# Reordering one core's instruction streams: batch 2's transposes, block 3's weight sums, and single copies and products

## The chip, the cores and the metric

One core of a Trainium2 chip runs the kernel. The metric is device time in microseconds of one execution; runs shown as times are medians. The engines are TensorE (PE, with its weight loads as PEld), VectorE (DVE), ScalarE (ACT), GpSimd (POOL) and SyncE (SP), whose queue issues most DMAs. Each engine executes its own instructions strictly in the order in which the kernel writes them, and waits on semaphores for the others.

## The reference

Eight batches of eight heads (sequence 576, head dimension 64) pass through a decayed linear attention; the result, 4608 tokens of width 512, goes through a feed-forward layer with a "snake" activation.

```python
scores = scale * np.matmul(q, k.transpose(0, 1, 3, 2))
Dmat = np.where(rel >= 0, gamma[:, None, None] ** rel[None, :, :], 0.0)
ret = scores * Dmat[None, :, :, :]
x = np.matmul(ret, v)              # to (tokens, 512)
h = x @ w_in                       # 512 -> 2048
s = np.sin(alpha * h)
g = h + s * s / (alpha + 1e-09)
out = g @ w_out                    # 2048 -> 512
```

## The kernel before

**Attention of one batch.** Queries and keys are loaded as float32 (`load`, L110, on SP's queue; the slots of the "raw" buffer are six), scaled by powers of gamma and cast to float16 (`cast`, L138, on DVE, POOL or ACT), and transposed: batches 0 and 1 on PE (`turn`, L209, then a copy out of PSUM, `take`), later batches by a DMA transpose on SP's queue (`crossed`, L201, L205). The 512 first tokens are cut into four chunks of 128. `outer` (L285, L298) makes the sum of key times value of each chunk; `evict` or `evict_bank` copies it from PSUM; `more` and `to_state` (L332 to L340, POOL) run the decayed sum over the chunks and cast the state. `scores` (L348, L358), `masked` (L366, L370, DVE), `values` (L378, L400) and `add_states` (L411, L422) give the output, which `keep` copies to `xT`. `values` is called twice for each half of the tokens (`same` false, then true), in matmuls on the two halves of the array's rows that write one bank. Between the two calls PE is drained (`change_rows`), or, with `relay`, a mark is queued on another engine that waits for the first group, and the second group waits for the mark (`told`, `order`).

**Feed-forward of one block of 512 tokens.** A unit is one of 16 slices of 128 of the 2048 hidden features. `project` (L527, L535) multiplies it on PE into a PSUM bank, `sine` (L540, ACT), `square` (L548, ACT mostly, DVE or POOL) and `product` (L557, L559, DVE) apply the activation and write `gT`; with the product the bank comes free. For blocks 0 and 1 `gemm2` (L576, L581) multiplies with `w_out` in 16 steps of four matmuls, and `finish` copies and stores. From block 2 on, class `Quarters` saves one of eight products of the second multiplication in the manner of Strassen and Winograd: weights are summed once (`weigh`, L602, POOL), and the activations of a block are summed as follows, each in two halves (0 and 1):

- `s3` (L618): a difference into the tile `d3`; read by `s2` and by multiplication 7
- `s1` (L621): in place; read by multiplication 5
- `s2` (L624) and `s4` (L630), both on POOL: in place; read by multiplications 1, 6 and 2, 3

`multiply` (L634, L652) makes one of the seven products; `add` (L665, L672, DVE) joins a product in PSUM with a stored sum and `store` writes out.

**Order.** Everything is written out by hand. Blocks 0 to 2 with the attention of batches 1 to 4 are one long list of calls (L750 to L1261). Blocks 3 to 7 come from a loop (L1276) in which the second multiplication of block n-1 (`Q`), the activation of block n (`N`), the scores and values of batch n+1 (`A`) and the casts, transposes and outer products of batch n+2 (`B2`) are laid between 16 units; the loop has conditions on `n == 3`, because block 3 follows the hand-written list. Three banks (h0, h1, h2) take turns for the units of the loop, so that unit u+3 needs the bank that the product of unit u frees. The bank "op" takes the second multiplication: multiplications 5 and 3 of one block fill it, an addition reads it, and multiplication 1 of the next block fills it anew.

Of the kernel before, what the change touches and what calls it, by code (L numbers as in the profile page):

```python
# [18 lines left out]
def kernel(  # L19
# [68 lines left out]
    V, A_, G_ = nc.vector, nc.scalar, nc.gpsimd  # L88
# [459 lines left out]
    def square(n, fc, eng):  # L548
        s_t = hps_of[n, fc][1]
        ss_t = work.tile([P, 512], F16, tag="ss", bufs=4, name="ss_t")  # L550
        if eng is nc.scalar:
            nc.scalar.activation(ss_t, s_t, mybir.ActivationFunctionType.Square)  # L552
        else:
            eng.tensor_tensor(ss_t, s_t, s_t, MULT)
        hps_of[n, fc][1] = ss_t

    def product(n, fc):  # L557
        hps, ss_t = hps_of.pop((n, fc))
        nc.vector.scalar_tensor_tensor(  # L559
            gT[n][:, :, fc, :], ss_t.rearrange("p (t n) -> p t n", t=2), inva[:, fc : fc + 1],  # L560
            hps.rearrange("p (t n) -> p t n", t=2), MULT, ADD,
        )
# [13 lines left out]
    def gemm2(n, u, tag, cols=slice(0, 512)):  # L576
        c, part = divmod(u, 4)
        if (n, c, cols.start) not in ops:
            ops[n, c, cols.start] = psum.tile([P, 512], F32, tag=tag, bufs=1, name="ops")
        for fk in range(4 * part, 4 * part + 4):  # L580
            matmul(  # L581
                ops[n, c, cols.start][:, cols], gT[n][:, c // 2, fk, c % 2 * P : c % 2 * P + P], w_out16[:, fk, cols],
                start=(fk == 0), stop=(fk == FC - 1), skip_group_check=True,
            )
# [102 lines left out]
    at = [Attention(b) for b in range(B)]  # L687
# [52 lines left out]
    with tc.manual_schedule():  # L740
# [139 lines left out]
        project(0, 11, "op")  # L880
        sine(0, 11)
        square(0, 11, V)
        product(0, 11)
        product(0, 10)
        turn(1, "k", 0, "m1")
        project(0, 12, "h2")
        sine(0, 12)
# [26 lines left out]
        at[1].scores(0, 1, "m1")  # L914
        at[1].masked(0, 0)
        at[1].masked(0, 1)
        gemm2(0, 13, "h2")
        cast(1, "v", 0, G_, (0,))
        cast(1, "v", 0, A_, (1,))
        load_w_out(2)  # L920
        load_w_out(3)
        gemm2(0, 1, "h0")
        load(2, "k", 1)
        load(2, "k", 0)
        load(2, "q", 0)
        at[1].outer((0,), "m0")
        at[1].evict((0,), A_)
        cast(1, "k", 1, G_)
        at[1].to_state(0, G_)
        at[1].values(0, False, "m1")  # L930
        at[1].values(0, True)
        turn(1, "k", 1, "h1")
        take(1, "k", 1, A_)
# [37 lines left out]
        finish(0, 1)  # L971
        cast(2, "q", 0, V)
        crossed(2, 0, "q")
        load(3, "k", 1)
        at[1].more(3)
        at[1].to_state(3, G_)
# [11 lines left out]
        sine(1, 1)  # L988
        gemm2(0, 3, "h0")
        product(1, 0)  # L990
        square(1, 1, A_)
        finish(0, 0)
        project(1, 2, "m1", 0)
        project(1, 2, "m1", 1)
        sine(1, 2)
# [1 line left out]
        square(1, 2, A_)  # L997
        project(1, 3, "h0")
        sine(1, 3)
        load(3, "q", 1)  # L1000
        load(3, "v", 0)
        crossed(2, 1, "k")
        crossed(2, 1, "q")
        load(3, "k", 0)
        load(3, "v", 1)
        load(3, "q", 0)
# [15 lines left out]
        sine(1, 6)  # L1022
        square(1, 6, A_)
        at[2].outer((0, 1), "op", "h2")
        at[2].evict_bank(0, V)
        project(1, 7, "h0", 0)
        project(1, 7, "h0", 1)
        at[2].evict_bank(1, V)
        project(1, 8, "h1", 0)
        project(1, 8, "h1", 1)  # L1030
        sine(1, 8)
# [204 lines left out]
        sine(2, 13)  # L1236
        square(2, 13, A_)
        product(2, 13)
        second[2].s3(1, V)
        sine(2, 14)  # L1240
        square(2, 14, A_)
        sine(2, 12)
        square(2, 12, V)
        product(2, 14)
        product(2, 12)
        project(2, 10, "h2", 0)
        project(2, 10, "h2", 1)
# [28 lines left out]
        for n in range(3, NBLK):  # L1276
            A = at[n + 1] if n < 7 else None
            B2 = at[n + 2] if n < 6 else None
            Q, N = second[n - 1], second[n]
            if n == 7:  # L1280
                E = (Ends(0), Ends(2))

            def scores(p):
                if A:
                    A.scores(p, 0, next(m))
                    A.scores(p, 1, next(m))
                elif n == 7 and p == 1:
                    E[0].scores(next(m))
                    E[1].scores(next(m))

            def masked(p, y):
                if A:
                    A.masked(p, y)
                elif n == 7 and p == 1:
                    E[y].masked()

            def values():
                if n == 7:
                    for e in E:
                        e.values(False, next(m))  # L1300
                    for e in E:
                        e.values(True)
                        e.add_states()
                    for e in E:
                        e.keep(0, A_)
                        e.keep(1, A_)
                if not A:
                    return
                relay = A_ if B2 else None
                A.values(0, False, next(m), relay=relay)  # L1310
                A.values(1, False, next(m), relay=relay)
                if B2:
                    B2.outer((0, 1), "op", next(h))
                A.values(0, True)
                A.add_states(0)
                A.values(1, True)
                A.add_states(1)
                if B2:
                    B2.evict_bank(0, A_)
                A.keep(0, A_)  # L1320
                if B2:
                    B2.evict_bank(1, A_)

            def begin(u):
                project(n, u, next(h))
                sine(n, u)

            def end(u):
                on_v = (12, 13) if A else ()
                square(n, u, V if u in on_v else A_)  # L1330
                product(n, u)

            def unit(u):
                begin(u)
                end(u)

            begin(0)
            if n < 6:
                for x in KEYS[3:]:
                    load(n + 2, *x)  # L1340
            if n == 6:
                last_tokens(1, "load")
                last_tokens(2, "load")
            if n == 7:
                last_tokens(3, "cast")
            if n > 3:
                Q.s1(0, V)
                Q.s1(1, V)
            end(0)
            unit(1)  # L1350
            Q.multiply(1, "X", "op")
            Q.keep("P1", "X")
            Q.s2(0, G_)
            Q.s2(1, G_)
            unit(2)
            begin(3)
            scores(0)
            end(3)
            masked(0, 0)
            masked(0, 1)  # L1360
            Q.multiply(2, "X")
            Q.keep("C11", "X")
            Q.store("C11", 0, 0)
            ahead = 3 if n == 3 else 6
            if n < 6:
                for x in KEYS[:ahead]:
                    cast(n + 2, *x, G_)
            Q.s4(0, G_)
            Q.s4(1, G_)
            if n < 6:  # L1370
                for x in KEYS[ahead:]:
                    cast(n + 2, *x, G_)
            if n == 6:
                for j in range(3):
                    last_tokens(j, "cast")
                last_tokens(3, "load")
            unit(4)
            begin(5)
            Q.multiply(6, "Y", "op")
            Q.add("U2", "P1", "Y")  # L1380
            end(5)
            if n == 3:
                Q.s1(0, V)
            unit(6)
            unit(7)
            if n == 3:
                Q.s1(1, V)
            Q.multiply(7, "Y")
            begin(8)
            scores(1)  # L1390
            Q.add("U3", "P1", "Y")
            masked(1, 0)
            end(8)
            masked(1, 1)
            if n < 5:
                for x in KEYS[:3]:
                    load(n + 3, *x)
            if n == 5:
                last_tokens(0, "load")
            unit(9)  # L1400
            begin(10)
            Q.multiply(4, "Y")
            Q.add("P1", "P1", "Y")
            Q.store("P1", 1, 0)
            end(10)
            if B2:
                crossed(n + 2, 0, "k")
                crossed(n + 2, 1, "k")
            N.s3(0, V)
            unit(11)  # L1410
            N.s3(1, V)
            begin(12)
            values()
            end(12)
            if B2:
                B2.chain((0, 1, 2, 3))
                crossed(n + 2, 0, "q")
                crossed(n + 2, 1, "q")
            begin(13)
            if A:  # L1420
                A.keep(1, A_)
            Q.multiply(5, "Z", "op")
            Q.add("U3", "U3", "Z")
            Q.store("U3", 1, 1)
            end(13)
            unit(14)
            begin(15)
            Q.multiply(3, "Z")
            Q.add("U2", "U2", "Z")
            Q.store("U2", 0, 1)  # L1430
            end(15)

        Q = second[8]
# [60 lines left out]
```

## Time and profile before

| | |
|---|---|
| median of three runs | 300.28 us (300.15 to 300.67) |
| profiled execution | 300.5 us, of which span 298.8 us |
| PE busy | 282.0 us (94% of the span) |
| DVE, ACT, POOL busy | 220.2, 210.3, 206.3 us |
| granted PE clock, mean | 0.995 |
| DMA | 49.89 MB, mean 167 GB/s |
| chain that ended last | 73% PE, 7% DVE, 6% POOL, 6% DMA |

All times of instructions are microseconds from the start of the span of the profiled execution. Busy time of PE is modelled from pipelined matmuls, so that "busy" does not mean "at its peak"; an idle gap of PE, on the other hand, is a wait. In rows of instructions a bracket gives the engine's idle time before the instruction and what ended it. Block 3 begins near 108 us and block 4 near 140 us.

### The profile page before, as it was taken

The page shows a single profiled execution, that of the slowest core. Times are in us where ns is not written, and L with a number is a line of the kernel's source. Part 1 is how long each engine was busy: PE and PEld are TensorE (multiplying, and loading weights), DVE is VectorE, ACT ScalarE, POOL GpSimd, SP SyncE. Part 2 cuts the span into 40 slices and gives each one's busy share as a digit, 9 for nine tenths or more (in the row PEclk, how much of TensorE's full clock was granted, in tenths as well). Part 3 has the DMA queues.
Part 4 walks back from the last instruction along what each step waited for, and adds up shares of the span by engine and source line. Part 5 has one row for each costly group of instructions (what it writes and reads, how often), then busy time and mean ns, then how long its engine had stood idle before and what let it go on. Part 6 is the DMA issues. An engine that isn't in the chain of part 4 may idle for free.

```text
span 298.8 us, 8739 instructions
## 1 busy us (share of the span) xinstructions
PE 282.0 (94%) x3599; PEld 183.3 (61%) x3599; DVE 220.2 (74%) x297; ACT 210.3 (70%) x338; POOL 206.3 (69%) x201
## 2 busy tenths in 40 slices
PE   7589999998899999989999999999999999999993
PEld 5454454575544576656666666766666666665782
DVE  3868957688768997998678667776778486656871
ACT  3559742795866898776878787878777878887600
POOL 4997869999799989887897799769925900370000
PEclk9999999999999999999999999999999999999998
DMA  8999999999999767988699786476648201310225
GB/s 227 291 241 216 254 217 284 255 253 159 221 273 300 90 152 174 259 191 197 143 260 185 173 203 174 88 160 145 159 91 192 55 0 41 71 37 18 61 49 120
DMA packets 119159, 49.89 MB, mean 167 GB/s; under 512 B 69824, under 2 KB 118096, under 8 KB 119120
## 3 DMA queue, kind: packets, MB, share of 16 engines
q1 hardware_dynamic: 114528, 45.04, 65.1%
q0 software_dynamic: 4224, 4.19, 8.4%
q8 instruction: 28, 0.46, 0.7%
q10 hardware_dynamic: 368, 0.11, 0.2%
q14 instruction: 11, 0.09, 0.1%
HBM read 36.74 MB, written 9.44 MB: 155 GB/s over the span
## 4 chain that ended last, share of the span: by engine, by line
PE 73%; DVE 7%; POOL 6%; DMA 6%; ACT 3%; issue 2%; SPq 1%; POOLq 0%; ACTq 0%; DVEq 0%
PE hps L535 33%; PE hps L652 27%; PE ops L581 5%; DMA q<-in_q_dram 5%; DVE ret L370 2%; DVE gT L559 2%; POOL T L602 2%; PE sc L358 2%; PE o L400 2%; PE idle L696 1%; POOL v L104 1%; ACT s_t L543 1%; PE kv L298 1%; DMA k<-in_k_dram 1%; DVE k L181 1%
## 5 line engine op out<-in xcount | busy, mean ns | idle before, releaser
L559 DVE SCALAR_TENSOR_TENSOR gT<-ss_t,inva,hps 128x512 f16<-128x512 f16 x144 | 105.3, 744 | 42.2 <-ACT ss_t L552 39.7
L543 ACT ACTIVATE s_t<-hps,alpha_t 128x512 f16<-128x512 f32 x144 | 96.7, 680 | 39.9 <-PE hps L535 39.6
L535 PE MATMUL hps<-xT,w_in 128*128 128x512 f16 (+1 forms) x592 | 121.3, 350 | 3.2 <-DVE gT L559 2.8
L535 PEld LDWEIGHTS <-w_in 128*128 128x128 f16 x656 | 62.8, 98 | 54.5 <-issue 4.3
L552 ACT ACTIVATE ss_t<-s_t 128x512 f16<-128x512 f16 x119 | 74.5, 630 | 3.3
L652 PEld LDWEIGHTS <-gT 128*128 128x128 f16 x656 | 63.9, 98 | 14.4
L624 POOL TENSOR_TENSOR gT<-gT,d 128x1024 f16<-128x1024 f16 x12 | 25.2, 2123 | 29.7 <-PE hps L652 28.6
L652 PE MATMUL hps<-T,gT 128*128 128x256 f16 x336 | 39.8, 273 | 0.0
L652 PE MATMUL hps<-w_out,gT 128*128 128x256 f16 x320 | 38.2, 273 | 0.0
L370 DVE TENSOR_TENSOR ret<-sc,mask 128x1024 f16<-128x1024 f32 (+1 forms) x32 | 34.9, 1115 | 3.0 <-PE sc L358 2.9
L672 DVE TENSOR_TENSOR osb<-osb,hps 128x512 f32<-128x512 f32 x35 | 24.0, 685 | 15.4 <-PE hps L652 14.7
L581 PE MATMUL ops<-w_out,gT 128*128 128x512 f16 x128 | 30.8, 380 | 0.0
L181 POOL TENSOR_TENSOR q<-q,cn 128x1024 f16<-128x1024 f32 (+1 forms) x16 | 25.7, 1622 | 1.5 <-DMA q<-in_q_dram 1.4
L630 POOL TENSOR_TENSOR gT<-gT 128x1024 f16<-128x1024 f16 x12 | 26.2, 2203 | 0.0
L332 POOL TENSOR_TENSOR s<-kvs,cn 128x256 f16<-128x256 f32 x24 | 15.5, 649 | 8.3 <-ACT kvs L102 7.5
L340 POOL TENSOR_TENSOR kvs<-s,kvs 128x256 f32<-128x256 f32 x24 | 19.1, 795 | 2.6 <-ACT kvs L102 0.9
L181 POOL TENSOR_TENSOR k<-k,cn 128x1024 f16<-128x1024 f32 (+1 forms) x11 | 18.5, 1686 | 1.3 <-DMA k<-in_k_dram 1.3
L581 PEld LDWEIGHTS <-gT 128*128 128x128 f16 x128 | 11.6, 98 | 12.7
L102 ACT COPY osb<-hps 128x512 f32<-128x512 f32 (+2 forms) x15 | 8.2, 548 | 13.7 <-PE hps L652 13.6
L102 ACT CAST xT<-o 128x1024 f16<-128x1024 f32 (+1 forms) x16 | 14.4, 910 | 4.4 <-PE o L422 4.4
L181 DVE TENSOR_TENSOR k<-k,cn 128x512 f16<-128x512 f32 (+1 forms) x11 | 13.3, 1228 | 4.9 <-DMA k<-in_k_dram 4.8
L339 POOL TENSOR_TENSOR s<-kvs,cn 128x256 f32<-128x256 f32 x24 | 16.4, 682 | 0.2
(74 smaller groups left out, 270.3 us busy)
## 6 DMA issues: line engine op xcount, KB each, us to landing
out_dram<-osb SPq DMA_DIRECT2D x70, 128.0 KB, 2.5
q<-in_q_dram SPq DMA_DIRECT2D x16, 512.0 KB, 5.6
k<-in_k_dram SPq DMA_DIRECT2D x10, 512.0 KB, 8.8
v<-in_v_dram SPq DMA_DIRECT2D x10, 512.0 KB, 7.5
k<-in_k_dram SPq DMA_DIRECT2D x24, 128.0 KB, 3.4
v<-in_v_dram SPq DMA_DIRECT2D x24, 128.0 KB, 3.4
w_in<-in_moe_w_in_dram POOLq DMA_DIRECT2D x4, 512.0 KB, 10.0
w_out<-in_moe_w_out_dram POOLq DMA_DIRECT2D x4, 512.0 KB, 11.4
```

Source lines behind the costliest of these rows:

```text
L102: eng.copy(d_, s_)
L181: return eng.tensor_tensor(dst[:, a0:a1].rearrange("p a r t d -> p t (a r) d"), t_.rearrange("p (t a) x -> p t a x", t=2)[:, :, a0:a1].rea ...
L370: nc.vector.tensor_tensor(ret.rearrange("p t (z x) -> p (t z) x", z=2)[:, :, 0:n], sc.rearrange("p t (z x) -> p (t z) x", z=2)[:, :, 0:n], ...
L535: matmul(hps_of[n, fc][0][:, cols], w_in16[:, a, fc * P : (fc + 1) * P], xs[n][:, a, cols], start=(a == 0 and part != 1), stop=(a == KT - ...
L543: nc.scalar.activation(s_t, hps, mybir.ActivationFunctionType.Sin, bias=0.0, scale=alpha_t[:, fc : fc + 1],)
L552: nc.scalar.activation(ss_t, s_t, mybir.ActivationFunctionType.Square)
L559: nc.vector.scalar_tensor_tensor(gT[n][:, :, fc, :], ss_t.rearrange("p (t n) -> p t n", t=2), inva[:, fc : fc + 1], hps.rearrange("p (t n) ...
L581: matmul(ops[n, c, cols.start][:, cols], gT[n][:, c // 2, fk, c % 2 * P : c % 2 * P + P], w_out16[:, fk, cols], start=(fk == 0), stop=(fk ...
L624: eng.tensor_tensor(self.part(0, 0, i), self.part(1, 1, i), self.d3[:, 4 * i : 4 * i + 4], SUB)
L630: eng.tensor_tensor(out_, self.part(1, 0, i), self.part(0, 0, i), SUB)
L652: matmul(self.ps[name][:, 256 * m + cols.start : 256 * m + cols.stop], left(j)[:, P * m : P * m + P], right(j)[:, cols], start=(tag is not ...
L672: nc.vector.tensor_tensor(out_, a, self.ps[ps], ADD)
```

## The change

Nothing is computed differently; calls move in the written order, and with them the instructions of each engine's queue.

1. Block 0: the product of unit 10 comes ahead of that of unit 11 (DVE).
2. Batch 1: one step of block 0's second multiplication moves from ahead of the first outer product to between the two groups of values; the two groups are separated by a mark on POOL in place of a drain of PE. The outer product and its chunk sums so come sooner.
3. Batch 2: the DMA transpose of the second half of k moves on SP's queue ahead of the load of batch 3's k, and that of q ahead of the load of batch 3's q. Before, both stood behind three of batch 3's six loads.
4. Block 1: the copy of block 0's first rows (`finish(0, 0)`) comes ahead of the square of unit 1 (ACT).
5. Batch 2: the two copies of the chunk sums change places (DVE).
6. Block 2's `s3(1)` moves from between the products of units 13 and 12 to behind block 3's unit 0; the product of unit 14 comes ahead of the square of unit 12 (DVE).
7. Block 3: POOL casts the second half of k after `s4(0)`, not before it, and the other three casts after `s4(1)`.
8. Block 3: `s1(1)` moves from behind unit 7 to behind unit 10, and the two `s3` of block 3 from behind units 10 and 11 to behind unit 14 (DVE).

```diff
-        product(0, 11)
         product(0, 10)
+        product(0, 11)
...
-        gemm2(0, 13, "h2")
         cast(1, "v", 0, G_, (0,))
         cast(1, "v", 0, A_, (1,))
         load_w_out(2)
         load_w_out(3)
-        gemm2(0, 1, "h0")
+        gemm2(0, 13, "h2")
...
         at[1].outer((0,), "m0")
         at[1].evict((0,), A_)
         cast(1, "k", 1, G_)
+        at[1].values(0, False, "m1", relay=G_)
+        gemm2(0, 1, "h0")
         at[1].to_state(0, G_)
-        at[1].values(0, False, "m1")
         at[1].values(0, True)
...
         crossed(2, 0, "q")
+        crossed(2, 1, "k")
         load(3, "k", 1)
...
         product(1, 0)
+        finish(0, 0)
         square(1, 1, A_)
-        finish(0, 0)
...
         sine(1, 3)
+        crossed(2, 1, "q")
         load(3, "q", 1)
         load(3, "v", 0)
-        crossed(2, 1, "k")
-        crossed(2, 1, "q")
         load(3, "k", 0)
...
-        at[2].evict_bank(0, V)
+        at[2].evict_bank(1, V)
         project(1, 7, "h0", 0)
         project(1, 7, "h0", 1)
-        at[2].evict_bank(1, V)
+        at[2].evict_bank(0, V)
...
         product(2, 13)
-        second[2].s3(1, V)
         sine(2, 14)
         square(2, 14, A_)
         sine(2, 12)
+        product(2, 14)
         square(2, 12, V)
-        product(2, 14)
         product(2, 12)
...
             end(0)
+            if n == 3:
+                Q.s3(1, V)
             unit(1)
...
-            ahead = 3 if n == 3 else 6
             if n < 6:
-                for x in KEYS[:ahead]:
+                for x in KEYS[: 2 if n == 3 else 6]:
                     cast(n + 2, *x, G_)
             Q.s4(0, G_)
+            if n == 3:
+                cast(n + 2, *KEYS[2], G_)
             Q.s4(1, G_)
-            if n < 6:
-                for x in KEYS[ahead:]:
+            if n == 3:
+                for x in KEYS[3:]:
                     cast(n + 2, *x, G_)
...
             unit(7)
-            if n == 3:
-                Q.s1(1, V)
             Q.multiply(7, "Y")
...
-            N.s3(0, V)
+            if n == 3:
+                Q.s1(1, V)
+            else:
+                N.s3(0, V)
             unit(11)
-            N.s3(1, V)
+            if n > 3:
+                N.s3(1, V)
...
             unit(14)
+            if n == 3:
+                N.s3(0, V)
+                N.s3(1, V)
             begin(15)
```

More of the change, by code (lines that the diff above doesn't have):

```diff
@@ L882 @@
         square(0, 11, V)
+        product(0, 10)
         product(0, 11)
-        product(0, 10)
         turn(1, "k", 0, "m1")
```

## The prediction

> **What bounds the kernel now.** I read the busy time by stretch first, then the waits of TensorE (PE), then the instructions around each wait in order of time. Columns by stretch: length, then busy us and instruction count of PE, weight loads, DVE, ACT, POOL; granted clock; DMA share; GB/s.
>
> ```profile
> 66.00:79.00 13.00, 10.76 (x194) 7.27 (x192) 9.96 (x13) 8.61 (x16) 11.33 (x14) 1.00 1.19 217
> 79.00:110.00 31.00, 30.74 (x427) 17.42 (x426) 25.89 (x31) 24.13 (x38) 30.13 (x33) 1.00 0.93 201
> ...
> 128.00:134.00 6.00, 4.56 (x167) 3.03 (x166) 6.00 (x8) 4.24 (x7) 5.54 (x5) 1.00 0.78 175
> 134.00:270.00 136.00, 135.90 (x1624) 90.80 (x1623) 97.75 (x140) 106.97 (x169) 89.83 (x73) 1.00 0.58 131
> ```
>
> From 134 us PE is busy 135.90 of 136 us: nothing is to be had there, and whatever PE gains before 134 us reaches the end unless another engine then comes late. What can be had is idle time before: 2.24 us in 66 to 79 and 1.44 us in 128 to 134. Between them (79 to 110) PE has 0.26 us idle, so a gain at 78 us also passes if POOL, busy 30.13 of 31 us there, moves with it.
>
> **Block 3: sums moved (units 0, 10, 11, 14).** PE first, then DVE, then POOL (start, duration, engine, line, operation; in brackets the engine's idle time before it and what ended that).
>
> ```profile
> 112.24 1.89 PE L535 MATMUL hps<-xT,w_in 128*128 128x512 f16 x8 [0.20 <-DVE gT L559]
> ...
> 130.03 1.02 PE L535 MATMUL hps<-xT,w_in 128*128 128x512 f16 x4 [0.66 <-DVE gT L559]
> ...
> 133.74 1.02 PE L535 MATMUL hps<-xT,w_in 128*128 128x512 f16 x4 [0.78 <-DVE gT L559]
> ...
> 141.57 1.91 PE L652 MATMUL hps<-w_out,gT 128*128 128x256 f16 x16
> ```
> ```profile
> 124.50 1.29 DVE L621 TENSOR_TENSOR gT<-gT 128x1024 f16<-128x1024 f16 x1
> ...
> 129.24 0.73 DVE L559 SCALAR_TENSOR_TENSOR gT<-ss_t,inva,hps 128x512 f16<-128x512 f16 x1
> ...
> 130.49 0.73 DVE L559 SCALAR_TENSOR_TENSOR gT<-ss_t,inva,hps 128x512 f16<-128x512 f16 x1
> 131.15 1.88 DVE L618 TENSOR_TENSOR d<-gT 128x1024 f16<-128x1024 f16 x1
> 132.95 0.73 DVE L559 SCALAR_TENSOR_TENSOR gT<-ss_t,inva,hps 128x512 f16<-128x512 f16 x1
> 133.61 1.06 DVE L618 TENSOR_TENSOR d<-gT 128x1024 f16<-128x1024 f16 x1
> ...
> 138.82 0.75 DVE L559 SCALAR_TENSOR_TENSOR gT<-ss_t,inva,hps 128x512 f16<-128x512 f16 x1 [0.36 <-ACT ss_t L552]
> 140.05 0.69 DVE L672 TENSOR_TENSOR osb<-osb,hps 128x512 f32<-128x512 f32 x1 [0.48 <-PE hps L652]
> ...
> 141.31 1.29 DVE L621 TENSOR_TENSOR gT<-gT 128x1024 f16<-128x1024 f16 x2
> ```
> ```profile
> 112.33 4.20 POOL L624 TENSOR_TENSOR gT<-gT,d 128x1024 f16<-128x1024 f16 x2 [1.08 <-DVE gT L559]
> ...
> 120.81 1.90 POOL L181 TENSOR_TENSOR k<-k,cn 128x1024 f16<-128x1024 f32 x1 [1.34 <-DMA k<-in_k_dram]
> ...
> 128.73 3.75 POOL L181 TENSOR_TENSOR q<-q,cn 128x1024 f16<-128x1024 f32 x2
> ```
>
> PE waits at 130.03 for the product of unit 9 and at 133.74 for that of unit 11, each of which frees a PSUM bank. Ahead of unit 9's product stands s1(1) (124.50, 1.29); ahead of unit 11's stands s3(0) (131.15, 1.88). DVE has no idle time in 128 to 134, so order decides.
> - s1(1) leaves unit 7: all DVE work up to unit 10's product comes up to 1.29 us sooner, unit 9's product ends near 128.7 (129.97 less 1.29) and PE needs it at 129.37 (130.03 less 0.66). The 0.66 goes.
> - In s3(0)'s place comes s1(1), at about 129.93 (131.22, the end of unit 10's product, less 1.29). It lasts 0.65 (mean of the two at 141.31, POOL idle) to 1.88 (the sum at 131.15, beside POOL's second q cast, which ended at 132.48). Unit 11's product then ends between 131.3 and 132.6; PE, its 0.66 saved, wants it at 132.3 (133.74 - 0.78 - 0.66). I take a remaining wait of 0.3: 0.48 of 0.78 goes. POOL's new order (s4(0) ahead of the k cast that waits 1.34 for its load) ends the casts about 1 us sooner, which favours the lower end.
> - s3(1) of batch 2 leaves the end of block 2, so unit 2's bank comes sooner and the 0.20 at 112.24 goes. It now runs after unit 0's product, just after the start of POOL's first s2 (112.33, half of 4.20). Bounds 0.65 and 1.88 again, or until that s2 ends plus 0.6, near 115.0. POOL's second s2 and DVE's product of unit 1 queue behind it; that product's bank is needed only by unit 4, behind two units, the scores and a whole multiplication (some 1.9 + 0.6 + 1.9 us of PE work after 112.2). Cost 0; it would cost once that product ended after 116.3.
> - Both s3 now stand after unit 14, in front of the addition at 140.05 whose bank the multiplication at 141.57 needs. Two sums of 0.65 starting at 139.57 (138.82 + 0.75) end at 140.9, the addition at 141.6: cost 0. At 1.06 each (133.61), the addition ends at 142.4: 0.8 lost. I take 0.2, since POOL is nearly done there (its next work in block 4 comes after the multiplication).
>
> The Trainium skill (SBUF — State Buffer, on engine ports) has DVE with two SBUF inputs and GpSimd take an exclusive port pair, the loser blocking for a whole instruction. By it s1(1), if it starts after the last q cast does, ends only about 0.55 after that cast; the trace agrees (131.15 plus 1.88 is 0.55 after 132.48). The sum by it would lose up to 0.6 of the 0.78, which lies inside my bounds.
>
> Block 3 in sum: 0.20 + 0.66 + 0.48 - 0.2 = 1.15 us, between 0.2 and 1.64.
>
> **Batch 2's second transposes (53 to 83 us).** SP's queue, the DMA rate in 40 slices of 0.5 us from 60 to 80, PE, POOL, and the chain's row for batch 3's last load:
>
> ```profile
> 58.78 0.58 SPq L121 DMA_DIRECT2D k<-in_k_dram  x1
> ...
> 61.36 0.80 SPq L121 DMA_DIRECT2D v<-in_v_dram  x1
> 62.20 6.74 SPq L205 DMA_TRANSPOSE kT<-k  x1
> 69.04 1.41 SPq L205 DMA_TRANSPOSE qT<-q  x1
> ```
> ```profile
> GB/s 80 74 193 315 361 391 269 285 308 260 225 295 327 275 191 44 7 13 22 22 95 286 228 212 43 219 334 325 326 330 339 368 324 337 380 321 226 55 39 307
> ```
> ```profile
> 69.38 1.03 PE L535 MATMUL hps<-xT,w_in 128*128 128x256 f16 x8 [0.93 <-DVE gT L559]
> ...
> 72.55 0.64 PE L358 MATMUL sc<-qT,kT 64*64 64x128 f16 x32 [0.41 <-DMA qT<-q]
> ...
> 77.91 0.32 PE L400 MATMUL o<-ret,v 64*64 64x128 f16 x9 [0.80 <-issue]
> ```
> ```profile
> 79.09 1.90 POOL L181 TENSOR_TENSOR q<-q,cn 128x1024 f16<-128x1024 f32 x1 [1.45 <-DMA q<-in_q_dram]
> ```
> ```profile
> 71.75 7.21 DMA q<-in_q_dram
> ```
>
> The k transpose sits 6.74 us on SP behind three loads, and from 67.5 to 70 the DMAs move 7 to 44 GB/s. With the k transpose ahead of load k and the q transpose ahead of load q, they can be issued at about 58.8 and 62 (two store issues and load k later), 3 and 7 us sooner, with one load in front in place of three. The 0.41 at 72.55 goes. Loads q and v slide back by two transposes (1.41 of issue each); their casts come later than either lands. Loads k, v, q behind them go up by the dead stretch, up to 2.5 us, so POOL's 1.45 before 79.09 shrinks.
>
> Two larger PE waits lie around it. The one at 77.91 starts in the middle of a run of like matmuls, with nothing to wait for; the product named at 69.38 had ended at 67.40 (second of the pair at 66.00, below). Both follow a 16 KB packet of the queue "instruction", one in 67 to 68.2 us and one in 75.7 to 76.8, with none in the 6 us before either:
>
> ```profile
> 66.00 1.40 DVE L559 SCALAR_TENSOR_TENSOR gT<-ss_t,inva,hps 128x512 f16<-128x512 f16 x2
> ```
> ```profile
> q8 instruction: 1, 0.02, 5.0%
> ```
> ```profile
> q8 instruction: 1, 0.02, 5.5%
> ```
>
> So I read both as PE waiting for its own code, late while the rings are full. If the code comes at the same time as now, the 0.41 only lengthens the wait at 77.91 and nothing is won; if it comes sooner, 0.41 + 0.93 + 0.80 = 2.14 goes. I take 0.6, nearer to 0 since the rings stay full in both orders.
>
> **Edits I cost at nothing.**
>
> ```profile
> 33.12 1.04 PE L535 MATMUL hps<-xT,w_in 128*128 128x512 f16 x4 [0.20 <-DVE gT L559]
> ...
> 42.91 0.31 PE L422 MATMUL o<-qT,s 64*64 64x128 f16 x8 [0.48 <-POOL s L332]
> ...
> 43.61 1.03 PE L581 MATMUL ops<-w_out,gT 128*128 128x512 f16 x4
> ...
> 56.91 1.89 PE L535 MATMUL hps<-xT,w_in 128*128 128x512 f16 x8 [0.17 <-ACT osb L102]
> ```
> ```profile
> 36.40 0.75 DVE L559 SCALAR_TENSOR_TENSOR gT<-ss_t,inva,hps 128x512 f16<-128x512 f16 x1
> ...
> 37.67 2.54 DVE L370 TENSOR_TENSOR ret<-sc,mask 128x1024 f16<-128x1024 f32 x2 [0.19 <-PE sc L358]
> ```
> ```profile
> 42.47 1.01 ACT L102 COPY kT<-tr 128x1024 f16<-128x1024 f16 x1 [0.30 <-PE tr L215]
> ```
>
> Product 10 ahead of 11 removes the 0.20 at 33.12, but the first scores of batch 1 need product 15's bank at 37.15 (36.40 + 0.75), the end of an unbroken DVE queue with the same content: 0. Batch 1: the outer product goes sooner by the moved gemm2 and the wait for the state at 42.91 (0.48) goes; but the values need the bank that masking frees at 40.21 (37.67 + 2.54), the k turn stays where it is, now behind the moved gemm2, and the gemm2 at 43.61 needs the bank that ACT's copy of that turn frees at 43.48 (42.47 + 1.01): 0, at most 0.1 either way. Its cover gone (a copy that starts sooner), it would win up to 0.48. The new POOL mark has to_state(0) queued behind it, which waits longer for ACT anyway. Finish ahead of square: PE's 0.17 at 56.91 goes; but the square and what ACT does behind it come later by the wait for gemm2's end, and the outer product of batch 2 needs a bank from a product behind ACT's queue, where I let the 0.17 come back: 0, between -0.17 and 0.17. Bank 1 before bank 0: PE's waits list none for those copies, so 0.
>
> **Sum.** The profiled execution took 300.5 us, 0.22 over the median. 300.5 - 1.15 - 0.6 = 298.75; against the median 298.5.
>
> **Rivals.**
> 1. Code-bound (0.15): the code packets keep their times, only block 3 counts: 300.28 - 1.15 = 299.1. For: the delays in 61 to 77. The Trainium skill (Runtime: NRT & Kernel Launch, instruction fetch mechanics) holds the crossing of a 16 KiB block mostly hidden; by it these two waits have another cause, which the change leaves, and the time is the same. The two packets above speak against that page.
> 2. Code early (0.15): all of 2.14 goes: 300.28 - 1.15 - 2.14 = 297.0. For: the dead stretch lies around the first packet.
> 3. Block 3 given back (0.12): the sums meet POOL at both new places and 0.95 returns: 299.5.
> 4. Slower (0.12): each transpose opens a dead stretch of its own. Then load q, last of batch 3, lands 2.5 later than 78.96, POOL's cast of it starts at 81.5 in place of 79.09, and the v casts queued behind and batch 3's outer product, which needs them, come 2.4 later: 300.28 + 2.4 - 1.15 = 301.5. It decides once that load lands after 80.4, the 1.45 used up. Against: fewer loads stand in front of either.
> 5. Nothing moves, the waits reappearing elsewhere at their old length (0.04): 300.3.
>
> **Numbers.** Forecast case 0.42, own range 297.7 to 299.2 (the bounds of the two terms, not all at once). The range 296.6 to 300.2 leaves out rival 4 and most of rival 5. Within 0.2% (0.6 us, about what a measurement of this kernel can tell) lie half of 3 (0.06), a little of 1 (0.02) and 5 (0.04): 0.12; slower is rival 4, 0.12; faster the rest, 0.76.
>
> **What would show it.** Right: no PE wait near 129 and under 0.4 near 132; no wait for qT at 72; POOL's wait for load q under 1 us; no new PE wait at 141. Wrong: PE waiting for an addition or a product at 139 to 145, the code packets later than now, or load q landing after 79.

## The result, and the profile after

Over 20 executions each the changed kernel took 299.31 us (297.72 to 301.62) and the kernel before 301.12 us (299.29 to 303.02). The ratio on record, by which the text goes, is 0.9952, interval 0.993 to 0.9974; the quotient of the two medians is 0.9940. The forecast stood at 0.9941 (298.5 / 300.28), inside that interval. The profiled execution took 298.65 us, of which span 296.9, where 298.75 was forecast for it. Single executions of either kernel differ by up to 4 us, so one profile shows where a wait is and a ratio shows what it is worth.

The busy time by stretch, columns as before the change:

```profile
66.00:79.00 13.00, 12.61 (x206) 8.32 (x204) 11.37 (x14) 9.77 (x18) 12.69 (x15) 1.00 0.95 247
79.00:110.00 31.00, 30.38 (x426) 17.37 (x425) 25.10 (x32) 23.81 (x39) 30.20 (x35) 1.00 0.86 196
128.00:134.00 6.00, 6.00 (x179) 4.30 (x178) 4.42 (x6) 5.09 (x8) 4.37 (x6) 1.00 0.78 176
134.00:270.00 136.00, 135.56 (x1615) 89.99 (x1613) 99.29 (x141) 107.04 (x170) 90.00 (x71) 1.00 0.58 130
```

PE's idle time falls from 2.24 to 0.39 us in 66 to 79 and from 1.44 to 0 in 128 to 134. In 79 to 110 it grows from 0.26 to 0.62.

Block 3 after, PE first, then DVE, then POOL:

```profile
111.33 1.98 PE L535 MATMUL hps<-xT,w_in 128*128 128x512 f16 x8
...
127.53 1.89 PE L535 MATMUL hps<-xT,w_in 128*128 128x512 f16 x8
...
131.39 1.02 PE L535 MATMUL hps<-xT,w_in 128*128 128x512 f16 x4
132.25 1.91 PE L652 MATMUL hps<-T,gT 128*128 128x256 f16 x16
...
139.58 1.91 PE L652 MATMUL hps<-w_out,gT 128*128 128x256 f16 x16 [0.21 <-DVE osb L672]
```
```profile
128.99 1.69 DVE L621 TENSOR_TENSOR gT<-gT 128x1024 f16<-128x1024 f16 x1
130.60 0.74 DVE L559 SCALAR_TENSOR_TENSOR gT<-ss_t,inva,hps 128x512 f16<-128x512 f16 x1
...
137.11 1.82 DVE L618 TENSOR_TENSOR d<-gT 128x1024 f16<-128x1024 f16 x2
138.85 0.67 DVE L672 TENSOR_TENSOR osb<-osb,hps 128x512 f32<-128x512 f32 x1
```
```profile
126.37 3.76 POOL L181 TENSOR_TENSOR q<-q,cn 128x1024 f16<-128x1024 f32 x2
...
137.15 1.23 POOL L340 TENSOR_TENSOR kvs<-s,kvs 128x256 f32<-128x256 f32 x1
```

The waits that stood at 112.24, 130.03 and 133.74 are gone: none of the first three rows has a bracket. One wait is new in this block, 0.21 for the addition at 138.85, which has both `s3` in front of it.

Batch 2 and 3: SP, PE, POOL.

```profile
57.78 1.31 SPq L205 DMA_TRANSPOSE kT<-k  x1
...
61.09 1.46 SPq L205 DMA_TRANSPOSE qT<-q  x1
```
```profile
72.35 0.64 PE L358 MATMUL sc<-qT,kT 64*64 64x128 f16 x32
...
75.77 1.38 PE L400 MATMUL o<-ret,v 64*64 64x128 f16 x64
```
```profile
75.71 4.21 POOL L181 TENSOR_TENSOR q<-q,cn 128x1024 f16<-128x1024 f32 x2
```

Both transposes are off SP in 1.31 and 1.46 us, where one took 6.74. The scores at 72.35 do not wait, the 64 matmuls at 75.77 run in one piece, and POOL casts q without idle time.

### The profile page after: what moved, and what is told of

It is laid out like the page before. It is cut to its first block, busy times and chain, and to the rows that moved or that the text cites. A ratio compares the mean times of both kernels' runs of the same rounds, so it can differ in the third digit from the quotient of the medians.

```text
span 296.9 us, 8741 instructions
## 1 busy us (share of the span) xinstructions
PE 283.8 (96%) x3599; PEld 184.6 (62%) x3599; DVE 218.3 (74%) x297; ACT 209.7 (71%) x338; POOL 206.9 (70%) x201
## 4 chain that ended last, share of the span: by engine, by line
PE 70%; POOL 11%; DVE 7%; DMA 4%; ACT 3%; issue 2%; SPq 2%; POOLq 0%; ACTq 0%
PE hps L535 31%; PE hps L652 28%; PE ops L581 3%; DVE gT L559 3%; POOL T L602 3%; PE sc L358 2%; DMA k<-in_k_dram 2%; PE o L400 2%; POOL kvs L340 2%; DMA v<-in_v_dram 2%; POOL q L181 1%; SPq L121 1%; POOL v L104 1%; ACT s_t L543 1%; POOL s L332 1%
## 5 line engine op out<-in xcount | busy, mean ns | idle before, releaser
L630 POOL TENSOR_TENSOR gT<-gT 128x1024 f16<-128x1024 f16 x12 | 25.3, 2128 | 0.0
L332 POOL TENSOR_TENSOR s<-kvs,cn 128x256 f16<-128x256 f32 x24 | 17.0, 710 | 7.3 <-ACT kvs L102 6.5
L340 POOL TENSOR_TENSOR kvs<-s,kvs 128x256 f32<-128x256 f32 x24 | 19.7, 819 | 3.3 <-ACT kvs L102 1.6
L339 POOL TENSOR_TENSOR s<-kvs,cn 128x256 f32<-128x256 f32 x24 | 15.6, 652 | 0.2
L535 PE MATMUL hps<-xS,w_in 128*128 128x512 f16 x64 | 15.0, 379 | 0.0
```

The source lines that it names most:

```text
L340: nc.gpsimd.tensor_tensor(self.kvs[:, c], s32, self.kvs[:, c], ADD)
L535: matmul(hps_of[n, fc][0][:, cols], w_in16[:, a, fc * P : (fc + 1) * P], xs[n][:, a, cols], start=(a == 0 and part != 1), stop=(a == KT - ...
L630: eng.tensor_tensor(out_, self.part(1, 0, i), self.part(0, 0, i), SUB)
```

## The experiments

The runs are compared by PE's time from one landmark to the next, in us between starts of PE rows. **Ahead** runs from batch 2's outer product (61.43 before) to block 3's first multiplication (110.13 before). **Block 3** runs from there to block 4's first multiplication (141.57 before). Its two later parts are **products** (second scores of the block to multiplication 5, with units 9 and 11) and **sums** (multiplication 5 to block 4's first, with unit 14). The products part of before, as an example, is the difference of these two starts:

```profile
124.29 0.64 PE L358 MATMUL sc<-qT,kT 64*64 64x128 f16 x32
...
134.60 1.58 PE L652 MATMUL hps<-T,gT 128*128 128x256 f16 x13
```

| run | edits | ahead | block 3 | products | sums | ratio, 95% |
|---|---|---|---|---|---|---|
| before | | 48.70 | 31.44 | 10.31 | 6.97 | |
| e6_before_again | none | 47.63 | 31.15 | 10.17 | 6.95 | one execution |
| e5_code_shift | none, PE's code shifted | 47.22 | 31.51 | 10.20 | 6.95 | one execution |
| e3_rest | 1, 2, 4, 5 | 47.31 | 31.63 | 10.22 | 6.95 | 0.9993 [0.9965, 1.0021] |
| e1_transposes | 3 | 48.09 | 31.68 | 10.37 | 6.94 | 1.0006 [0.9979, 1.0033] |
| e2_block3 | 6 to 8 | 47.68 | 29.98 | 8.78 | 7.33 | 0.9974 [0.9941, 1.0006] |
| e4_t_b3 | 3, 6 to 8 | 49.31 | 29.98 | 8.77 | 7.33 | 0.9962 [0.9939, 0.9986] |
| after | all | 47.31 | 30.00 | 8.78 | 7.33 | 0.9952 [0.993, 0.9974] |
| after_again | all | 47.21 | 30.03 | 8.83 | 7.32 | 0.9957 [0.9922, 0.9993] |
| e8_s3_only | `s3` of 8 | 48.01 | 30.73 | 9.37 | 7.33 | one execution |
| e9_s1_only | `s1` of 8 | 48.00 | 30.66 | 9.68 | 6.95 | one execution |
| e10_s3_split | 6 to 8, `s3` apart | 47.73 | 30.01 | 9.14 | 6.94 | 0.9953 [0.9925, 0.998] |
| e7_v_first | 3 with v first, 6 to 8 | 47.22 | 30.03 | 8.82 | 7.33 | 0.9951 [0.9929, 0.9974] |
| e11_all | as e7, `s3` apart | 47.98 | 30.01 | 9.14 | 6.94 | 0.9942 [0.9919, 0.9965] |

Each ratio is against executions of the kernel before that ran beside that kernel (their medians are 300.23 to 301.12). The columns of block 3 repeat to a few tenths whatever else is changed. The column "ahead" does not: with one and the same instruction order it is 48.70 and 47.63.

**The transposes alone.** The kernel before with edit 3 of the change and no other.

> The kernel before with the two moved transposes of batch 2 alone. Theory (the new order of SP's queue brings PE's code and batch 3's last load sooner): PE's waits at 69.4 (0.93), 72.5 (0.41) and 77.9 us (0.80) are gone, POOL's 1.45 us in front of the q cast too, batch 3's outer product starts 1.5 to 2 us sooner, and the time is 1.2 to 2 us shorter (ratio 0.993 to 0.996); block 3's waits at 130 and 133.7 stay. Rival (the code packets came sooner by chance or through the other edits): the two code waits stay near 0.9 and 0.8, and under 0.5 us is won.

Measured 300.39 against 300.23 us, where 1.2 to 2 us less were expected. What was expected at its own place came: the waits at 69.4, 72.5 and 77.9 are gone, POOL's 1.45 too, and the outer product of batch 3 comes at 81.19 in place of 82.07. The time did not follow. What is late next, PE's rows of this run:

```profile
102.70 1.47 PE L535 MATMUL hps<-xT,w_in 128*128 128x512 f16 x8 [0.36 <-DVE gT L559]
...
127.02 1.91 PE L652 MATMUL hps<-T,gT 128*128 128x256 f16 x16 [0.51 <-DVE osb L672]
...
130.60 1.02 PE L535 MATMUL hps<-xT,w_in 128*128 128x512 f16 x4 [0.77 <-DVE gT L559]
```

PE ends at 293.59 against 293.75 in the profile of before. With the sums of block 3 in their old places, block 3 took 31.68, longer than before's 31.44: a gain of this size does not show at the end.

**Block 3 alone.** Edits 6, 7 and 8.

> The kernel before with the moved sums and casts of blocks 2 and 3 alone. Theory: PE's waits at 112.2 (0.20), 130.0 (0.66) and 133.7 (0.78) go, a wait of 0.2 to 0.4 for the addition appears at the start of block 4, and the time is 1.0 to 1.5 us shorter (ratio 0.995 to 0.997). Rival (the sums meet POOL at their new places): waits of together 0.9 or more appear between 112 and 146 us and under 0.5 us is won.

Measured 298.76 against 300.23 us, ratio 0.9974; its interval reaches 1.0006, so that the time alone does not show the gain, and the profile has to. Block 3 took 29.98, 1.46 less than before, with this trace's PE:

```profile
127.21 1.89 PE L535 MATMUL hps<-xT,w_in 128*128 128x512 f16 x8
...
131.07 1.02 PE L535 MATMUL hps<-xT,w_in 128*128 128x512 f16 x4
...
139.26 1.91 PE L652 MATMUL hps<-w_out,gT 128*128 128x256 f16 x16 [0.22 <-DVE osb L672]
```

The waits go without the transposes too.

**The four small edits alone.** Edits 1, 2, 4 and 5.

> The kernel before with the four small edits alone (product order, batch 1's outer product, finish ahead of square, order of the two bank copies). Prediction's step: nothing, within 0.2 us. Theory after the trace of the changed kernel, in which batch 2's outer product comes 0.84 us later: they cost 0.3 to 0.8 us (ratio 1.001 to 1.003), of which the finish ahead of the square delays the products of block 1 by 0.1 to 0.2 us and the rest comes from a state that waits for POOL.

Measured 300.16 us, ratio 0.9993: no difference. This zero is a sum and not four zeros. PE's waits of 0.48 and 0.17 (in before at 42.91 and 56.91) stand in all eleven profiles without these edits and in none of the three with them (e3 and both of after); the 0.20 at 33.12 is gone in the three and in three of the eleven. Two others stand in these three and in none of the eleven (PE's rows of e3):

```profile
43.22 1.02 PE L581 MATMUL ops<-w_out,gT 128*128 128x512 f16 x4 [0.31 <-ACT kT L102]
...
61.41 0.71 PE L298 MATMUL kv<-v,k 64*64 64x64 f16 x64 [0.50 <-DVE gT L559]
```

The first is for the copy by ACT that the prediction named; 0.17 of the 0.48 was won, where it allowed 0.1. The second is the 0.17 that it let come back, and it came back as 0.50. Batch 2's outer product so starts at 61.41 against 61.43.

**Transposes and block 3 together.**

> The changed kernel without the four small edits: transposes and block 3 only. If the two large parts add up and the small edits cost 0.3 to 0.8 us, the time is 2.2 to 3 us under the kernel before (ratio 0.990 to 0.993) and below the changed kernel. If the small edits are worth nothing, the ratio is that of the changed kernel, 0.995; if the two large parts share one gain, it is no better than the better of them.

Measured 298.83 us, ratio 0.9962: not apart from block 3 alone (0.9974), and not the 0.990 to 0.993 that two full gains would have made. The profiled execution, though, shows a wait that the forecast had excluded. ACT, then PE:

```profile
72.36 0.62 ACT L102 CAST v<-v 128x512 f16<-128x512 f32 x1 [1.47 <-DMA v<-in_v_dram]
```
```profile
76.61 1.38 PE L400 MATMUL o<-ret,v 64*64 64x128 f16 x64 [1.24 <-DVE ret L370]
...
102.40 0.93 PE L400 MATMUL o<-ret,v 64*64 64x128 f16 x32 [1.00 <-DVE gT L559]
```

The load of batch 3's v, which had slid back behind a transpose, landed after ACT wanted it, and the values came 1.24 late. The row at 102.40 is taken up below.

**Before once more.** A second profile of the unchanged kernel, to see which waits belong to the order and which to one execution.

> The kernel before, unchanged, profiled once more. Theory (the waits of 0.93 and 0.80 us at 69.4 and 77.9 us belong to that one execution, because its two code packets came late): they are absent or much shorter, the packets start within 3 us of the place where the others do, the wait for the q transpose (0.4 to 0.6) and block 3's waits (0.2, 0.66, 0.78) are there again, and batch 3's outer product starts near 81. Rival (they belong to the order of the loads): both waits return at 0.7 or more.

The wait in the middle of the values is there again (PE's rows), the ones at 69.38 and 72.55 are not:

```profile
77.00 1.26 PE L400 MATMUL o<-ret,v 64*64 64x128 f16 x55
79.16 0.32 PE L400 MATMUL o<-ret,v 64*64 64x128 f16 x9 [0.89 <-issue]
```

PE stood 2.02 us later at batch 2's outer product (63.45 against 61.43), enough for qT to arrive in time. Of the 2.02, 1.28 were there when batch 1's k was transposed (31.01 against 29.73): the granted clock was 0.73 from 10 to 20 us and 0.93 from 20 to 30, where the first profile has 1.00, and the first 32 matmuls of values (L400) took 1.38 in place of 0.92. A wait of 0.55 for POOL's state at 52.28 is new too.

**v ahead of q.** As e4, with batch 3's first load of v ahead of its first load of q.

```diff
         crossed(2, 1, "q")
-        load(3, "q", 1)
         load(3, "v", 0)
+        load(3, "q", 1)
```

> Transposes and block 3 as in the changed kernel, without the small edits, and batch 3's load v in front of load q. Theory (the transposes win 0.4 to 0.6 at the scores and give it back where ACT's v cast waits for a load that now stands behind two transposes): ACT's wait for load v (1.47 us in the same kernel with q first) is gone, the matmuls of values follow the scores in 3.6 us or less, and the time is 0.3 to 0.8 us below that kernel (ratio to before 0.993 to 0.995). Rival (the load's place is not what gave it back): ACT or PE still waits 1 us between 70 and 78, ratio 0.996.

Measured 299.26 against 300.74 us, ratio 0.9951. ACT's cast of v starts without a wait (its row of this run):

```profile
71.57 0.61 ACT L102 CAST v<-v 128x512 f16<-128x512 f32 x1
```

In the profiles of after it had no wait either, so this shows that the load can be made early, not that the time needs it.

**The two moves of block 3 apart.** Before with only the two `s3` moved behind unit 14 (e8), and with only `s1(1)` moved behind unit 10, in front of the `s3(0)` that stays (e9).

```diff
-            N.s3(0, V)
+            if n > 3:
+                N.s3(0, V)
             unit(11)
-            N.s3(1, V)
+            if n > 3:
+                N.s3(1, V)
...
             unit(14)
+            if n == 3:
+                N.s3(0, V)
+                N.s3(1, V)
```

> The kernel before with block 3's two s3 alone moved behind unit 14; s1(1) stays behind unit 7. From batch 4's second scores to multiplication 5 the kernel before takes 10.31 us and the changed one 8.78. Theory (each sum holds up the product behind it): the wait for unit 9's product stays at 0.6 to 0.8, that for unit 11's goes, so 9.3 to 9.6; and from multiplication 3 to block 4's multiplication 1 it takes 3.85 in place of 3.47, the wait for the addition. Rival (POOL's order of casts is what counts): 10.0 or more.

> The kernel before with s1(1) alone moved behind unit 10, directly in front of block 3's first s3, which stays. Theory: the wait for unit 9's product (0.66) goes, but two sums now stand in front of unit 11's product, so that wait grows from 0.78 to between 1.4 and 2.6, and the stretch from batch 4's second scores to multiplication 5 stays at 10.0 to 11.0 us: the two moves are worth something only together. Rival (the moves are worth their own share each): 9.6 or less.

PE of e8, then of e9:

```profile
129.94 1.02 PE L535 MATMUL hps<-xT,w_in 128*128 128x512 f16 x4 [0.49 <-DVE gT L559]
...
132.86 1.04 PE L535 MATMUL hps<-xT,w_in 128*128 128x512 f16 x4
...
141.06 1.91 PE L652 MATMUL hps<-w_out,gT 128*128 128x256 f16 x16 [0.21 <-DVE osb L672]
```
```profile
128.36 1.89 PE L535 MATMUL hps<-xT,w_in 128*128 128x512 f16 x8
...
133.12 1.02 PE L535 MATMUL hps<-xT,w_in 128*128 128x512 f16 x4 [0.90 <-DVE gT L559]
```

In e8 unit 9's wait stays and unit 11's goes, with the products at 9.37. In e9 unit 9's wait goes and unit 11's grows only from 0.78 to 0.90, with the products at 9.68: less than the 10 to 11 that I had expected. DVE of e9 shows why:

```profile
129.82 1.98 DVE L621 TENSOR_TENSOR gT<-gT 128x1024 f16<-128x1024 f16 x1
131.73 0.68 DVE L618 TENSOR_TENSOR d<-gT 128x1024 f16<-128x1024 f16 x1
```

Whichever sum stands beside POOL's last q cast takes long; the one behind it takes 0.68. The two moves win 0.94 and 0.63 in the products with POOL's casts in their old order, and all of edits 6 to 8 win 1.53. No run moved the casts alone.

**PE's code shifted.** Before, with the first `keep_busy` as 32 matmuls of half the width in place of 16, so that PE's code has 32 more matmuls at its start.

```diff
-        keep_busy(16, "h0", 256)
+        keep_busy(32, "h0", 128)
```

> The kernel before with 32 more PE instructions at its start (16 warming matmuls of 256 columns become 32 of 128, their work unchanged), so that every block of PE's code begins 32 instructions earlier in the program. Theory (PE waits for its own code): a wait inside the values of batch 2, if it comes (it did in four of six looks at the old order of loads), stands 32 instructions earlier, after about 7 of the second group's 32 matmuls in place of 23, and ends 1.1 to 1.3 us after a code packet. Rival (something in that group of matmuls): it stays after 23. If no packet is late, there is no wait and the run tells nothing apart.

No wait in the middle of the values, and its code packet began at 68.75. But e2 and e3, with the old order and their code not shifted, had theirs at 69.19 and 69.05 and no such wait either. The run tells nothing apart.

**The two `s3` apart.** Block 3's edits with the second `s3` of block 3 behind the addition, in front of unit 15's product.

```diff
             unit(14)
             if n == 3:
                 N.s3(0, V)
-                N.s3(1, V)
             begin(15)
             Q.multiply(3, "Z")
             Q.add("U2", "U2", "Z")
+            if n == 3:
+                N.s3(1, V)
```

> Block 3's change alone (old place of the transposes), with block 3's second s3 behind the addition that follows it, not in front. Theory (one sum less stands in front of the addition whose bank block 4's first multiplication needs): from multiplication 3 to block 4's multiplication 1 it takes 3.47 us in place of 3.85, the waits at 112 to 134 stay gone, and the time is 1.5 to 1.9 us under the kernel before (ratio 0.994 to 0.995). Rival (the sum then delays block 4's first products): that stretch or the next one (19.85 us to batch 6's outer product) is 0.3 us longer, and nothing is won against block 3's change alone (0.997).

Measured 299.29 against 300.32 us, ratio 0.9953. The wait for the addition is gone (sums 6.94), but this trace has a new one for unit 11's product:

```profile
132.50 1.02 PE L535 MATMUL hps<-xT,w_in 128*128 128x512 f16 x4 [0.39 <-DVE gT L559]
```

The products took 9.14 in place of 8.78, and block 3 30.01 in place of 29.98. e11, with the same split, has 9.14 too. The later product goes back to POOL, here in e10 and then in e2:

```profile
112.27 2.13 POOL L624 TENSOR_TENSOR gT<-gT,d 128x1024 f16<-128x1024 f16 x1 [1.18 <-PE hps L652]
...
127.49 3.76 POOL L181 TENSOR_TENSOR q<-q,cn 128x1024 f16<-128x1024 f32 x2
```
```profile
110.85 2.13 POOL L624 TENSOR_TENSOR gT<-gT,d 128x1024 f16<-128x1024 f16 x1 [0.61 <-PE hps L652]
...
126.05 3.76 POOL L181 TENSOR_TENSOR q<-q,cn 128x1024 f16<-128x1024 f32 x2
```

The first `s2` of the block starts 1.97 us after multiplication 1 in e10 (110.30) and 1.57 in e2 (109.28), and the last q cast keeps that distance (127.49 less 112.27 is 15.22, 126.05 less 110.85 is 15.20). Both lie ahead of the first instruction that the split moves, so the 0.36 can't be the split's own work; but e11 has 1.97 too, and the five profiles without the split 1.57 to 1.62. What differs stands just ahead of that `s2`: a square on DVE beside a row of POOL, in e10 and then in e2.

```profile
109.72 0.61 POOL L332 TENSOR_TENSOR sS<-kvs,cn 128x256 f16<-128x256 f32 x1
109.81 0.81 DVE L554 TENSOR_TENSOR ss_t<-s_t 128x512 f16<-128x512 f16 x1
```
```profile
108.77 0.42 DVE L554 TENSOR_TENSOR ss_t<-s_t 128x512 f16<-128x512 f16 x1
108.82 0.84 POOL L332 TENSOR_TENSOR sS<-kvs,cn 128x256 f16<-128x256 f32 x1
```

In e10 POOL starts 0.09 sooner and DVE's square takes 0.81; in e2 DVE starts 0.05 sooner and the square takes 0.42, POOL's row 0.84. The products that the `s2` waits for are behind the square on DVE. In e11 the square takes 0.81 as well, in the five without the split 0.42 to 0.46. So the 0.36 goes with which of the two engines starts first, ahead of the split, and the split's own part in the profiles is the 0.38 of the sums; the ratios (0.9953 against 0.9974, with intervals that overlap) do not show it in the time.

**All that helped, and the changed kernel again.**

> Transposes moved, load v in front of load q, block 3's change with its second s3 behind the addition, without the four small edits. If each part is worth what its stretch shows (0.4 to 1.2 us before batch 3's outer product, 1.4 in block 3, 0.4 at its end), the time is 2.0 to 2.8 us under the kernel before (ratio 0.991 to 0.9935) and 0.3 to 1 us below the changed kernel.

> The changed kernel once more, beside the others on one chip: ratio 0.995 to the kernel before. Theory (with the transposes in front, PE's code is early): no wait of PE inside the values of batch 2, and the code packet near 70 us starts within 2.5 us of the others of that order.

Measured 298.45 (0.9942 [0.9919, 0.9965]) and 299.01 us (0.9957 [0.9922, 0.9993]). For e11 0.991 to 0.9935 was expected, so the parts did not add up in full; its trace has the wait in the values again (1.22) and one of 1.13 for a load of w_out at 47.41. The intervals overlap nearly whole: e11 is the lowest median here and not shown to be faster than the change.

## Why the prediction was right, step by step

**Block 3: the mechanism holds; the gain was mis-sized by 0.3.** Forecast 0.20 + 0.66 + 0.48 - 0.2 = 1.14 (the prediction has 1.15); the profiles give 31.44 - 30.00 = 1.44. First multiplication to first scores: 3.92 to 3.66, 0.26 for 0.20. The products: 1.53 for 0.66 + 0.48. The step that failed there is the remaining wait of 0.3 at 132: `s1(1)` began at 128.99, ended at 130.68, and unit 11's product was done at 131.34, the lower end of what I had worked out (131.3 to 132.6, against 132.3 when PE wants it: the 0.3 was the upper end). POOL's casts ended at 130.13, 2.35 sooner than before (PE stood 0.82 sooner at the second scores), and not about 1. The casts' new order is not all of it: e9 has the old order, and its casts end at 131.26, 1.22 sooner than before's, with PE at the same place (second scores at 124.30 and 124.29). The sums: 0.36 lost, for 0.2. There "POOL is nearly done" failed: POOL's row at 137.15 ends at 138.38, and the two `s3` end 0.55 later. The five profiles with edits 6 to 8 as they are have 29.98 to 30.03, the five with none of them 31.15 to 31.68, so rival 3 (0.95 given back) and rival 5 are out.

**The ports.** `s1(1)` in after ended 0.55 us after POOL's cast (130.68 and 130.13); in e9 0.54 (131.80 and 131.26). The Trainium skill (SBUF — State Buffer, "SBUF: two separate sides") has the loser of the shared pair block for a whole instruction, and these rows agree. The prediction's "up to 0.6 of the 0.78" for this case does not come out of its own rows: with the last cast ending at 132.48, as before, 0.55 more is 133.03 for `s1(1)` and 133.68 for unit 11's product, 1.4 after the 132.3 at which PE wants it. It did not come to that because the cast had moved too.

**Batch 2's transposes: the local steps held, the 0.6 was not shown.** The transposes left SP early, the 0.41 for qT went, POOL's 1.45 is gone in after, and load q landed near 75.6 (issued at 68.29, 7.3 to landing), so rival 4 did not come. But edit 3 alone gave 1.0006, with 0.6 won only at the end of its interval (0.9979 of 300.23), and "ahead" has a median of 47.7 in the eight profiles with the old order and 47.6 in the six with the new one. Two steps failed.

First, "a gain at 78 us also passes if POOL moves with it". POOL moved; what was late next was a load, that of the first half of batch 4's v. ACT's row of before, then of after with the row behind it, then DVE and PE of after:

```profile
96.97 1.04 ACT L102 CAST v<-v 128x1024 f16<-128x1024 f32 x1 [0.47 <-DMA v<-in_v_dram]
```
```profile
97.33 1.04 ACT L102 CAST v<-v 128x1024 f16<-128x1024 f32 x1 [1.92 <-DMA v<-in_v_dram]
98.28 0.62 ACT L552 ACTIVATE ss_t<-s_t 128x512 f16<-128x512 f16 x1
```
```profile
98.94 0.75 DVE L559 SCALAR_TENSOR_TENSOR gT<-ss_t,inva,hps 128x512 f16<-128x512 f16 x1 [1.08 <-ACT ss_t L552]
```
```profile
101.20 0.93 PE L400 MATMUL o<-ret,v 64*64 64x128 f16 x32 [0.45 <-DVE gT L559]
```

PE was 1.08 us sooner at batch 3's outer product (80.99 against 82.07), and the load landed no sooner: SP issued it at 92.68 against 92.77, in both behind four stores. ACT waited for it with a square queued behind, DVE for the square, PE for a product of DVE. All 14 profiles agree: in the six where ACT waits 1.1 us or more for this load (e1, e4, e5, e7 and both of after), PE waits 0.36 to 1.00 near 101 to 103, and from batch 3's outer product to block 3's first multiplication it takes 28.45 to 28.96; in the other eight ACT waits at most 0.6, and that stretch takes 27.77 to 28.07. Five of the six have the new order. e5 has the old one, so the order is not needed for it; e3, in the old order too and with PE earlier still (80.79), waits only 0.59, so an early PE alone does not bring it either. Whether the new order holds this load back stays open. No run moved the load, so what it is worth was not tried.

Second, load v and load q "come later than either lands" in their casts: true in after, false in e4 (1.47 of ACT's wait, 1.24 of PE's).

**The code waits: seen again, cause not settled.** The wait inside the values came with a late code packet in before, e6, e8, e9, e10 (old order) and e11 (new order), 0.80 to 1.25 long; it was absent in e2, e3, e5 (old) and e1, e4, e7 and both of after (new). Where it is absent the packet began at 68.75 to 70.92, where it is present at 75.75 to 76.75. The packet before that one was late already: it began at 58.72 to 65.30 in the eight and at 65.72 to 67.18 in the six. The Trainium skill (Runtime: NRT & Kernel Launch, "Instruction fetch mechanics") holds such crossings mostly hidden. Eight of 14 profiles agree; in the other six PE stops, and no run shows that the code is what stops it. Five of eight against one of six leans to the order, but e11 and the three old ones show that the order does not decide, and the runs do not show what does. The wait of 0.93 at 69.38 appeared in no other run. So the two waits that I priced at up to 1.73 together were partly this one execution's, and rival 2 (297.0) stays unsupported: after's ratio makes 298.8 of the 300.28.

**In sum.** PE's end came 1.83 us sooner in the profiles (291.92 against 293.75): "ahead" gave 1.39, block 3 gave 1.44, batch 2's outer product came 0.84 later (62.27 against 61.43), and what lies behind block 3 took 0.16 more. The 0.84 is not the small edits' own: e6, with none, has 63.45, and e3, with all four, 61.41. Against e3, after is 0.20 later when batch 1's k is transposed (29.93 against 29.73, with a granted clock of 0.83 from 10 to 20 us against 1.00), and then waits 0.38 for a product at 37.41 and 0.27 for POOL's state at 50.97, of which e3 has neither. The small edits' sum of 0 agrees with e3's 0.9993. The forecast's 1.75 consisted of a term that was 0.3 too small and one that was 0.6 too large on what the runs show, and block 3's 1.44 alone is what the ratio on record moved (0.0048 of 301.12 is 1.45, between 0.78 and 2.11 by its interval), while the medians themselves moved 1.81. That the total fits is thus partly luck: one term was too small where the other was too large. Rival 1's end, only block 3 counting, describes the sum as well as the forecast case does, and the intervals don't separate them; its reason, code packets that keep their times, is not what the traces show.

Of the signs named in advance, the one at the addition (no new PE wait) failed, by 0.21, so that one of the three signs of being wrong came, small. The rest came as named.

## What to carry to other kernels

When sums share an engine with products that free banks, ask which of them stands beside the other engine's long operation: in e9 that sum took 1.98 us and the one behind it 0.68. Moving either sum won 0.94 or 0.63 of the 1.53; what moving the other engine's operation is worth by itself was not tried. A wait removed early is worth only what the next load lets through, so look beyond the engines to the loads that do not move with the work. And profile the unchanged kernel twice before pricing a wait whose cause the profile does not name: 0.93 of what I priced did not come back.

## What the runs showed of the hardware

- In six of 14 profiles PE stopped inside a run of like matmuls for 0.80 to 1.25 us, and in each it went on 1.2 to 1.5 us after a 16 KB code packet had landed (before: landed at 76.71, on at 77.91; e6: 77.71 and 79.16). That the packet is the cause is not shown.
- A transpose queued behind three loads held SP for 2.89 (e5) to 6.74 us (before) in the eight profiles with the old order; ahead of the three the same one took 1.29 to 1.31 us in the six with the new one.
- A sum on DVE that began beside a cast of POOL ended 0.54 to 0.55 us after the cast (after, e9). Of a square on DVE and a row of POOL that began within 0.1 us of each other, the later one took longer: 0.81 in place of 0.42 for the square (e10 and e2), 0.84 in place of 0.61 for POOL's row (e2 and e10).
- In six of 14 profiles the granted clock fell below 1.00 somewhere in the first 30 us, among them e6 (0.73 from 10 to 20 us), whose instructions are those of before, which has 1.00 there.
- Executions of the same instructions differ by up to 4 us (after: 297.72 to 301.62). Of two profiles each, block 3 differs by 0.03 (after: 30.00 and 30.03) and 0.29 (before: 31.44 and 31.15), and the start of batch 2's outer product by 0.54 (62.27 and 62.81) and 2.02 (61.43 and 63.45).
